# Normalising products of a fused attention and dense kernel placed on GpSimd or VectorE by the planner, with nine thresholds and a reserve table set anew

## Chip, cores and metric

The kernel runs on one core of one Trainium2 chip. The metric is device time in microseconds (us) of one execution. The engines go by the names of the profile: PE (TensorE, matrix products), PEld (its weight loads), ACT (ScalarE), DVE (VectorE), POOL (GpSimd) and SP (SyncE, which issues most DMAs).

## What is computed

The output mixes an attention and a dense block by a gate that is worked out for each token:

```python
g = sigmoid((x * gate_w).sum(-1, keepdims=True))
a = attention(x, wqkv, wo)         # S=2048, D=640, 32 heads of 20, softmax over all keys
b = (h * tanh(softplus(h))) @ w2   # h = x2 @ w1 + b1, F=1536
out = g * a + (1 - g) * b
```

All inputs and the output are bf16.

## The kernel before

The heads go in eight groups of four (g = 0 to 7), the queries in four chunks of 512 (c = 0 to 3). For each pair of chunk and group there are 16 tiles of 128 keys and four heads, and each of these units is one 128 x 512 block of scores in a bank of PSUM. Three units make a slot; there are 683 slots, and all engines work to the beat of the slots.

In a slot PE makes the three blocks of scores (line 1204), into banks 0 to 2 and 3 to 5 by turns, so that the scores of slot s+2 need the banks of slot s. ACT takes their exponentials in one instruction (line 1226), and writes them into ETS as bf16. In most slots only two of the three blocks go to ACT: the third is taken by DVE, which evicts it from PSUM as a 16-bit integer (line 1271, called an eviction here). Up to four such blocks of one group make a batch, and DVE turns a batch into exponentials with three more steps from SBUF to SBUF (line 1335 fraction, line 1339 product, line 1343 power). PE then multiplies the exponentials with the values (line 1463, PV) and gathers the result of the group in one bank, ACC. When a group is done, DVE copies ACC into OUNG (line 1545), the four rows of sums go out and come back through DMAs and a reciprocal (lines 1548 to 1559), spread over the partitions as BCT, and the normalising product OUNG times BCT is written to OTN or QT (line 1513). There are 32 groups, and one of them, the last, goes in two halves by its own code (lines 1532 to 1538); 31 products are made by line 1513.

Beside this, PE has tasks that share one bank, FB: projections of queries, keys and values (lines 598, 667, 795, 822), the hidden layer (950), its second product (1024), the output projection (1048). The bank is evicted by DVE after each task. ACT also makes 24 tanh (line 983) for the hidden layer, and DVE eight steps of the activation for each (lines 1005 and 1008).

The order of all of this on every engine is fixed before the kernel runs. A planner (class `Plan`, function `attention`) keeps a planned clock for each engine, adds each instruction with a planned cost, and decides from its clocks and from thresholds what comes next: `choose` decides for each slot whether its third block goes to DVE, `work` puts pieces of batches, activations and normalising steps into gaps of DVE, `pick` and the loop over `step` choose PE's tasks by due times, `emit_pv` decides when PV is issued, `fill_up` adds PE work that nobody needs (lines 1204 and 1743 again) where PE would idle. So a threshold changes no instruction's work, but which instruction stands where. At run time every engine works through its own list in order, and waits on semaphores for what its next instruction needs.

The functions that the change touches:

Of the kernel before, what the change touches and what calls it, by code (L numbers as in the profile page):

```python
# [14 lines left out]
ALU = mybir.AluOpType  # L15
# [22 lines left out]
OLD = 3  # L38
# [11 lines left out]
HOP = 0.1  # L50
# [5 lines left out]
STREAM = 0.5  # L56
SPUN = 0.65
EXP_PAIR = 0.908
WIDE = 0.60
QUICK = 0.335  # L60
FAST = 0.335
# [9 lines left out]
CHAIN = 2.6  # L71
# [8 lines left out]
AHEAD = 14  # L80
SPREAD = 3
# [7 lines left out]
CROWD = 1.4  # L89
MARGIN = 2.5  # L90
EAGER = 20
# [6 lines left out]
LAG = 5  # L98
SPARE = 7
WINDOW = 3.41  # L100
CALM = 3
PACKED = 10
PACKED_Q = 15
Q_AT = 100
# [26 lines left out]
WARM = 7  # L131
MORE = 8
# [11 lines left out]
class Plan:  # L144
# [3 lines left out]
    def __init__(self, prefix):  # L148
        self.prefix = prefix
        self.ops = []  # L150
        self.now = {e: 0.0 for e in ENGINES}
        self.kind = None
        self.passes = deque()
        self.queue = 0.0

    def add(self, eng, fn, deps=(), slot=None, cost=0.1, kind="F", tail=None, bulk=0.0):
# [86 lines left out]
def bass_gated_mix__softmax_full_mha__dense_activation_mish__prompt_kernel(  # L243
# [142 lines left out]
    def attention(pl, fast):  # L386
# [56 lines left out]
        def dve(fn, deps=(), cost=0.1, kind="F"):  # L443

            ready = max([pl.now["dve"], *(d.t1 + HOP for d in deps if d is not None)])
            work(ready + (LATER if fast and now["rate"] < BUSY and now["bank"] else SLACK))
            return pl.add("dve", fn, deps, cost=cost, kind=kind)
# [72 lines left out]
        if fast:  # L520
# [457 lines left out]
            def mish(ev, hb, hc, k):  # L978
# [9 lines left out]
                def piece(cost, fn, after=None):  # L988
                    def run():
                        last[0] = pl.add("dve", fn, [last[0]], cost=cost)  # L990
# [289 lines left out]
        def dve_by(fn, deps, cost, slack):  # L1280
# [3 lines left out]
            return pl.add("dve", fn, deps, cost=cost)  # L1284

        def close(batch):
# [15 lines left out]
            def piece(cost, fns, deps, after=None, split=False):  # L1302

                def run(some, each, mark):
                    def go():
                        for sp in some:
                            op = pl.add("dve", fns(sp), deps(), cost=each)
# [57 lines left out]
        def choose(s):  # L1365

            late = max(0.0, pl.now["dve"] - pl.now["act"])
# [132 lines left out]
        def group_done(c, g, step, last):  # L1500
# [11 lines left out]
            def times(src, deps):  # L1512
                oung_free[0] = bc_read[0] = otn_done[(c, g)] = pl.add("dve", lambda e: e.tensor_tensor(
                    otn(c, g, fast), src, BC, ALU.mult), [*deps, *reads()], cost=WIDE)
# [42 lines left out]
            def spread():  # L1557
# [5 lines left out]
                norm.append((WIDE, lambda: times(src, wide), lambda: wide[-1]))  # L1563
# [3 lines left out]
        if fast:  # L1567
# [9 lines left out]
            for g in range(NG):  # L1577
                for c in range(NC):
                    due = slot_of(0, g, 4 * c)
                    if c or g:  # L1580
# [4 lines left out]
                        if g == 0:  # L1585
                            tasks.append(kq_task(0, g, c, slot_of(1, 0, 0) - 5 if c < 2 else Q_AT + Q_STEP * (c - 2)))
# [418 lines left out]
```

## Time and profile before

| What | Value |
|---|---|
| median of 3 runs | 793.59 us (791.81 to 795.25) |
| the profiled execution | 791.41 us, span 789.5 us |
| busy: ACT, DVE, PE, POOL | 773.3, 748.3, 716.4, 8.0 us |
| exponentials of three blocks, of two blocks | 281, 402 |
| mean granted clock of TensorE | 0.999 |

The span runs from the first to the last instruction; 1.9 us of the execution lie around it. "Busy" merges instructions that overlap: an instruction starts before the one ahead of it has drained, so a group's mean duration is longer than the time from one start to the next, and a short wait hides under the drain. A row of the timeline gives start, length, engine, line, operation, tiles and count, and in brackets the idle time before it and what ended that. A row of groups ends with busy time, mean ns of one, and the idle time of the engine before the group.

### The profile page before, as it was taken

The page shows a single profiled execution, that of the slowest core. Times are in us where ns is not written, and L with a number is a line of the kernel's source. Part 1 is how long each engine was busy: PE and PEld are TensorE (multiplying, and loading weights), DVE is VectorE, ACT ScalarE, POOL GpSimd, SP SyncE. Part 2 cuts the span into 40 slices and gives each one's busy share as a digit, 9 for nine tenths or more (in the row PEclk, how much of TensorE's full clock was granted, in tenths as well). Part 3 has the DMA queues.
Part 4 walks back from the last instruction along what each step waited for, and adds up shares of the span by engine and source line. Part 5 has one row for each costly group of instructions (what it writes and reads, how often), then busy time and mean ns, then how long its engine had stood idle before and what let it go on. Part 6 is the DMA issues. An engine that isn't in the chain of part 4 may idle for free.

```text
span 789.5 us, 16459 instructions
## 1 busy us (share of the span) xinstructions
PE 716.4 (91%) x6690; PEld 262.7 (33%) x6690; DVE 748.3 (95%) x1313; ACT 773.3 (98%) x715; POOL 8.0 (1%) x14
## 2 busy tenths in 40 slices
PE   8999999889989888999999889999889899999995
PEld 4333333233323332233323233333333333333332
DVE  4889999999999999999999999999999999999995
ACT  6999999999999999999999999999999999999995
POOL 3000000000000000000000000000000000000000
PEclk9999999999999999999999999999999999999999
DMA  8731310211223221402111131202121213010001
GB/s 194 122 74 56 103 51 15 83 54 59 74 89 111 84 64 45 133 17 64 33 29 52 52 90 36 64 19 61 31 85 49 82 48 85 15 28 24 29 15 39
DMA packets 78184, 48.50 MB, mean 61 GB/s; under 512 B 23965, under 2 KB 73749, under 8 KB 78053
## 3 DMA queue, kind: packets, MB, share of 16 engines
q1 hardware_dynamic: 77700, 47.18, 22.2%
q8 instruction: 56, 0.92, 0.5%
q0 software_dynamic: 112, 0.01, 0.1%
q14 instruction: 28, 0.22, 0.1%
q10 hardware_dynamic: 288, 0.16, 0.1%
HBM read 37.64 MB, written 7.52 MB: 57 GB/s over the span
## 4 chain that ended last, share of the span: by engine, by line
ACT 91%; PE 5%; DVE 2%; DMA 1%; issue 0%; SPq 0%; POOL 0%; POOLq 0%
ACT ETS L1226 89%; ACT REG L983 2%; PE PS L1204 2%; PE PS L1463 1%; ACT W2R L983 1%; DMA WOQ<-in_A_wqkv_dram 1%; PE PS L822 0%; PE PS L598 0%; PE PS L667 0%; PE PS L1048 0%; DVE HB L1054 0%; PE PS L758 0%; PE PS L865 0%; PE PS L950 0%; DVE U L1005 0%
## 5 line engine op out<-in xcount | busy, mean ns | idle before, releaser
L1226 ACT ACTIVATE ETS<-PS 128x1024 bf16<-128x1024 f32 (+1 forms) x683 | 753.9, 1370 | 2.7 <-PE PS L1204 2.7
L1204 PE MATMUL PS<-QT,KT 32*128 32x512 bf16 (+1 forms) x2116 | 268.1, 378 | 55.7 <-ACT ETS L1226 46.3
L1463 PE MATMUL PS<-ETS,V_all 128*21 128x512 bf16 (+1 forms) x1699 | 161.8, 375 | 0.0
L1204 PEld LDWEIGHTS PS<-QT,KT 32*128 32x128 bf16 x2116 | 67.2, 91 | 281.4 <-ACT ETS L1226 254.5
L1271 DVE TENSOR_SCALAR PADS<-PS 128x512 int16<-128x512 f32 x97 | 66.3, 685 | 8.5 <-PE PS L1204 8.2
L1271 DVE TENSOR_SCALAR QT<-PS 128x512 int16<-128x512 f32 x102 | 69.7, 685 | 3.9 <-PE PS L1204 3.3
L1024 PE MATMUL PS<-W2R,HB 128*128 128x320 bf16 x384 | 68.5, 302 | 0.7 <-DVE HB L960 0.5
L1271 DVE TENSOR_SCALAR OTN<-PS 128x512 int16<-128x512 f32 x84 | 57.5, 686 | 0.6 <-PE PS L1204 0.5
L950 PE MATMUL PS<-XB,REG 128*128 128x256 bf16 x360 | 53.6, 275 | 2.3 <-DVE OUTT L1054 1.4
L1463 PEld LDWEIGHTS PS<-ETS,V_all 128*21 128x21 bf16 x1699 | 41.9, 91 | 41.2 <-issue 27.1
L1008 DVE TENSOR_TENSOR U<-U 128x1024 f16<-128x1024 f16 x72 | 49.4, 685 | 0.3
L1024 PEld LDWEIGHTS PS<-W2R,HB 128*128 128x128 bf16 x384 | 30.8, 98 | 32.4 <-issue 19.7
L950 PEld LDWEIGHTS PS<-XB,REG 128*128 128x128 bf16 x360 | 29.2, 97 | 25.8 <-issue 23.4
L960 DVE TENSOR_TENSOR HB<-PS,B1T 128x512 bf16<-128x512 f32 x48 | 32.9, 686 | 0.5 <-PE PS L950 0.3
L1005 DVE TENSOR_SCALAR U<-U 128x1024 f16<-128x1024 f16 x72 | 30.2, 420 | 0.4
L1743 PE MATMUL PS<-KT 128*128 128x512 bf16 x92 | 27.3, 384 | 0.0
L1048 PE MATMUL PS<-WOQ,QT 128*128 128x320 bf16 x128 | 24.5, 303 | 2.3 <-DVE HB L1054 0.6
L1271 DVE TENSOR_SCALAR REG<-PS 128x512 int16<-128x512 f32 x38 | 25.8, 685 | 0.2
L1048 PE MATMUL PS<-WOQ,OTN 128*128 128x320 bf16 x128 | 23.8, 302 | 0.1
L667 PE MATMUL PS<-XB,REG 128*128 128x512 bf16 x80 | 23.0, 383 | 0.2 <-DVE WOQ L676 0.2
L822 PE MATMUL PS<-REG,XB 128*128 128x160 bf16 (+1 forms) x240 | 23.1, 234 | 0.0
L667 PE MATMUL PS<-XB,WOQ 128*128 128x512 bf16 x80 | 22.8, 384 | 0.0
(187 smaller groups left out, 809.0 us busy)
## 6 DMA issues: line engine op xcount, KB each, us to landing
REG<-in_B_w_dram SPq DMA_DIRECT2D x36, 320.0 KB, 3.2
BCT<-SUMS SPq DMA_DIRECT2D x124, 64.0 KB, 2.1
W2R<-in_B_w_dram SPq DMA_DIRECT2D x12, 320.0 KB, 3.5
KT<-KS SPq DMA_DIRECT2D x28, 128.0 KB
QT<-QS SPq DMA_DIRECT2D x112, 20.0 KB
QS<-WOQ SPq DMA_DIRECT2D x16, 128.0 KB, 1.7
KS<-OTN SPq DMA_DIRECT2D x16, 128.0 KB, 1.7
W2R<-in_B_w_dram SPq DMA_DIRECT2D x1, 1920.0 KB, 9.8
```

What stands on the lines that cost most here:

```text
L667: return lambda e, bank: e.matmul(PS[:, bank, :], W[:, f, base:base + P], xt(c)[:, f, :], start=(f == 0), stop=(f == NFT - 1))
L950: return lambda e, bank: e.matmul(PS[:, bank, i * HW:(i + 1) * HW], w1b(n1)[:, f, i * P:(i + 1) * P], xt(c)[:, f, cols], start=(f == 0), s ...
L960: ev = dve(lambda e: e.tensor_tensor(hb, PS[:, bank, :].rearrange("p (i t) -> p i t", i=2), bias, ALU.add), [last, b_load, *guarded, *b_re ...
L1005: return lambda e: e.tensor_scalar(dst, src, *ops)
L1008: return lambda e: e.tensor_tensor(dst, one, two, ALU.mult)
L1024: return lambda e, bank: e.matmul(PS[:, bank, 0:HALF], HB[:, hc % 2, f, t * P:(t + 1) * P], W2[:, f, half * HALF:(half + 1) * HALF], start ...
L1048: return lambda e, bank: e.matmul(PS[:, bank, 0:HALF], otn(c, g, fast)[:, t * P:(t + 1) * P], WOG[:, g, half * HALF:(half + 1) * HALF], st ...
L1204: op = pl.add("pe", lambda e, i=i, g=real(g), tile=tile, j=j, cols=cols, c=c, of_q=of_q: e.matmul(scores(s)[:, i, cols], KT[32 * j:32 * j ...
L1226: e_op[s] = pl.add("act", lambda e: e.activation(ETS[:, s % NETS, 0:n, :], scores(s)[:, 0:n, :], AF.Exp, scale=SCALE, bias=LIFT if fast el ...
L1271: ev = dve_by(lambda e: e.tensor_scalar(block(batch["y"], n, I16), scores(s)[:, 2, :], SCALE * ULPS, BIAS, ALU.mult, ALU.add), [s_op[s], * ...
L1463: lasts[n] = pl.add("pe", lambda e, v=v, j=j, src=src[:, cols], of_q=of_q, count=count: e.matmul(PS[32 * j:32 * j + EW, ACC, of_q], v, src ...
L1743: pl.add("pe", lambda e: e.matmul(PS[:, bank, :], k[:, 0:P], k, start=True, stop=True), [free], cost=PASS, kind="S")
```

## The change

It has three parts.

First, the normalising product of a group (line 1513) can be made by POOL. The planner notes every planned DVE instruction with its end and a mark "L" on those that work from SBUF to SBUF in batches, activations and products (`kind="L"`). After each instruction planned through `dve` or `dve_by`, the new function `settle` looks whether the product that waits next could begin on POOL behind the last marked instruction, when its DMA has landed, and end while DVE's planned list still holds unmarked ones. If so the product goes to POOL, and waits for the DVE instruction just ahead of that point. If not, and 4 us (`AWAIT`) of planned time have gone by since its DMA landed, DVE makes it as before.

Second, nine thresholds get new values: how old an exponential may get before its PV is issued regardless of the scores (`OLD` 3 to 2), how dense PE's stream must be (`STREAM`), the planned cost of closing a batch (`CHAIN`), how early forced tasks of PE are begun (`AHEAD`, `SPREAD`) and other tasks may be brought forward (`EAGER`), how much of DVE's other work counts when a batch is judged tight (`CROWD`), how late tasks may be (`LAG`), and the first slot in which DVE may take a block (`CALM`). The first two tasks of queries for group 0 are due 10 slots (`LEAD`) instead of 5 ahead of their need.

Third, a table with one entry for 8 slots (`NUDGE`) is taken off the planned lateness of DVE in `choose`, which makes it more or less willing to give DVE a block there.

```diff
-OLD = 3
+OLD = 2
-STREAM = 0.5
+STREAM = 0.48
+ASIDE = 1.35
+APART = 0.1
+AWAIT = 4
-CHAIN = 2.6
+CHAIN = 3.0
-AHEAD = 14
-SPREAD = 3
+AHEAD = 20
+SPREAD = 4
-CROWD = 1.4
+CROWD = 1.1
-EAGER = 20
+EAGER = 45
-LAG = 5
+LAG = 14
-CALM = 3
+CALM = 2
+LEAD = 10
+NUDGE = [0, 0, 0, 0, 0, 0, 0, 0, 0, 0, -0.5, 0, 0, 0, 0, 0, 0, 1, 0, 0, 0, 0, 0, 2, 1, 0, 0, 0, 0, 0, 0, 0, 2, 0, 0, 0, 0, -1, 0.5, 3, 0, 1, 0, 0, 0, 0, 0, 0, 1, 0, 0, 0, 0, 0, 0, -1, 0, 0, 0, 0, 2, 2, 0, 0.5, 0, 0, 0, 0, 0, 3, -0.5, -0.5, 2, 0, 1, 0, 0, 0, 0, 0, 0, -0.5, 0.5, 0.5, 1, 3]
...
+        if eng == "dve":
+            self.line.append((at + cost, op, kind == "L"))
...
+        def settle():
+
+            if norm and len(norm[0]) > 3:
+                ready, put = norm[0][3]
+                line = pl.line
+                i = len(line)
+                while i and not line[i - 1][2]:
+                    i -= 1
+                begin = max(ready.t1 + HOP, pl.now["pool"], line[i - 1][0] if i else 0.0)
+                while i < len(line) and line[i][0] <= begin:
+                    i += 1
+                if begin + ASIDE + APART <= pl.now["dve"]:
+                    norm.popleft()
+                    put(line[i - 1][1])
...
-            late = max(0.0, pl.now["dve"] - pl.now["act"])
+            late = max(0.0, pl.now["dve"] - pl.now["act"]) - NUDGE[s // 8]
...
-            def times(src, deps):
-                oung_free[0] = bc_read[0] = otn_done[(c, g)] = pl.add("dve", lambda e: e.tensor_tensor(
-                    otn(c, g, fast), src, BC, ALU.mult), [*deps, *reads()], cost=WIDE)
+            def times(src, deps, eng="dve"):
+                oung_free[0] = bc_read[0] = otn_done[(c, g)] = pl.add(eng, lambda e: e.tensor_tensor(
+                    otn(c, g, fast), src, BC, ALU.mult), [*deps, *reads()], cost=WIDE if eng == "dve" else ASIDE, kind="L")
...
-                norm.append((WIDE, lambda: times(src, wide), lambda: wide[-1]))
+                if fast:
+                    norm.append((WIDE, lambda: times(src, wide), lambda: pl.now["dve"] > wide[-1].t1 + AWAIT and wide[-1],
+                                 (wide[-1], lambda dep: times(src, [*wide, dep], "pool"))))
+                else:
+                    norm.append((WIDE, lambda: times(src, wide), lambda: wide[-1]))
...
-                            tasks.append(kq_task(0, g, c, slot_of(1, 0, 0) - 5 if c < 2 else Q_AT + Q_STEP * (c - 2)))
+                            tasks.append(kq_task(0, g, c, slot_of(1, 0, 0) - LEAD if c < 2 else Q_AT + Q_STEP * (c - 2)))
```

What the planner makes of it is seen in the lists of the engines. Lines of the changed kernel are higher by 25 to 31, so line 1513 of before is 1540, 1204 is 1229, 1271 is 1296, 1335, 1339 and 1343 are 1362, 1366 and 1370, 1463 is 1490, and 1054 is 1079. In both kernels ACT's list has 281 exponentials of three blocks, 402 of two blocks and 24 tanh, in another sequence; DVE's has 401 evictions in both. DVE's list has 31 normalising products before and 18 now; the batches are 113 before and 119 now (line 1335, or 1362). Counted by width, a fraction or a power is 2048 wide in 91 batches before and 89 now, 1024 in 15 and 15, 512 in 7 and 15; the products of line 1339 are 38 of 2048, 121 of 1024 and 7 of 512 before, and 40, 113 and 15 now.

On POOL, from the copy of the gate's weights (line 615) to the end of the kernel, the list of the changed kernel now reads:

```order
L615 COPY REG<-OUTT 128x5
L1540 TENSOR_TENSOR OTN<-OUNG,BCT 128x512 x2
L1701 TENSOR_LOAD FLAG
L1701 ISA x2
L1540 TENSOR_TENSOR OTN<-OUNG,BCT 128x512 x5
L1540 TENSOR_TENSOR QT<-OUNG,BCT 128x512 x6
L1903 TENSOR_TENSOR HB<-PADS,W2R 128x320
```

The 13 rows of line 1540 are new; before, POOL had nothing there but the load of a flag and the last row.

On PE, near slot 17, the list of before had a task of values (line 795), one slot's scores, and at once a task of queries (line 598, XB with WOQ), which uses the same bank:

```order
L1463 MATMUL PS<-ETS,V_all 21x512 x7
L795 MATMUL PS<-REG,XB 128x80 x20
L1204 MATMUL PS<-QT,KT 128x512 x3
L598 MATMUL PS<-XB,WOQ 128x512 x5
L1204 MATMUL PS<-QT,KT 128x512 x6
L1463 MATMUL PS<-KT,V_all 21x512 x3
```

In the changed kernel the same task of queries (now line 623) stands a few slots earlier, and its neighbours are others:

```order
L1229 MATMUL PS<-QT,KT 128x512 x3
L820 MATMUL PS<-REG,XB 128x80 x20
L1229 MATMUL PS<-QT,KT 128x512 x6
L1490 MATMUL PS<-ETS,V_all 21x512 x6
L623 MATMUL PS<-XB,WOQ 128x512 x5
L1229 MATMUL PS<-QT,KT 128x512 x6
L623 MATMUL PS<-XB,REG 128x512 x5
```

Two slots' scores and six matmuls of PV now stand between the task of values and that of queries, where one slot's scores stood.

On DVE, near the end, before the last half group is normalised, the list of before had ended its last batch (line 1343) ahead of the half group's copy (line 1530):

```order
L1339 TENSOR_TENSOR OTN<-OTN 128x2048
L1054 SCALAR_TENSOR_TENSOR W2R<-PS,GATE,XB 128x320
L1343 TENSOR_SCALAR OTN<-OTN 128x2048
L1054 SCALAR_TENSOR_TENSOR W2R<-PS,GATE,XB 128x320
L1513 TENSOR_TENSOR QT<-OUNG,BCT 128x512
L1530 COPY OUNG<-PS 128x256
L1532 STREAM_TRANSPOSE BCT<-OUNG 128x256
```

In the changed kernel a whole batch (three rows of lines 1362, 1366 and 1370) stands behind the half group's product (line 1565):

```order
L1540 TENSOR_TENSOR QT<-OUNG,BCT 128x512
L1557 COPY OUNG<-PS 128x256
L1559 STREAM_TRANSPOSE BCT<-OUNG 128x256
L1560 RECIPROCAL RR<-BCT 128x8
L1561 STREAM_TRANSPOSE BCT<-RR 128x256
L1565 TENSOR_TENSOR QT<-OUNG,BCT 128x256
L1362 TENSOR_SCALAR OTN<-REG 128x2048
L1079 SCALAR_TENSOR_TENSOR W2R<-PS,GATE,XB 128x320
L1366 TENSOR_TENSOR OTN<-OTN,REG 128x2048
L1079 SCALAR_TENSOR_TENSOR HB<-PS,GATE,W2R 128x320
L1370 TENSOR_SCALAR REG<-REG 128x2048
```

So one more batch is worked off in the last ten slots, and the block it needs is evicted later than the last one was before.

More of the change, by code (lines that the diff above doesn't have):

```diff
@@ L153, in __init__ @@
         self.passes = deque()
+        self.line = []
         self.queue = 0.0
@@ L989, in run @@
                     def run():
-                        last[0] = pl.add("dve", fn, [last[0]], cost=cost)
+                        last[0] = pl.add("dve", fn, [last[0]], cost=cost, kind="L")
                         if after:
@@ L1306, in go @@
                         for sp in some:
-                            op = pl.add("dve", fns(sp), deps(), cost=each)
+                            op = pl.add("dve", fns(sp), deps(), cost=each, kind="L")
                         if mark:
```

8 lines of the change are left out of this document (6 added, 2 removed).

## The prediction

> **What bounds the kernel now.** First the busy time of each engine, from the page, and the chain of work that ended last:
>
> ```profile
> PE 716.4 (91%) x6690; PEld 262.7 (33%) x6690; DVE 748.3 (95%) x1313; ACT 773.3 (98%) x715; POOL 8.0 (1%) x14
> ACT 91%; PE 5%; DVE 2%; DMA 1%; issue 0%; SPq 0%; POOL 0%; POOLq 0%
> ```
>
> ACT is busy for 773.3 of 789.5 us, and 91% of the last chain is ACT: from its first exponential on the kernel is as long as ACT's list. DVE, with 748.3 us, is the next. So the first question is whether the change shortens ACT's list. These are its groups by form, from the view of groups:
>
> ```profile
> L1226 ACT ACTIVATE ETS<-PS 128x1536 bf16<-128x1536 f32 x281 | 446.9, 1621 | 2.2 <-PE PS L1204 2.2
> L1226 ACT ACTIVATE ETS<-PS 128x1024 bf16<-128x1024 f32 x402 | 441.5, 1194 | 0.5 <-PE PS L1204 0.5
> L983 ACT ACTIVATE REG<-HB 128x1024 f32<-128x1024 bf16 x18 | 22.3, 1239 | 0.0
> L983 ACT ACTIVATE W2R<-HB 128x1024 f32<-128x1024 bf16 x6 | 7.3, 1220 | 0.0
> ```
>
> The durations there overlap (1.621 and 1.194 us hold the drain), so I take the time from start to start. The timeline of ACT has two stretches between tanh, and the groups of these stretches tell what is in them:
>
> ```profile
> 458.18 1.07 ACT L983 ACTIVATE REG<-HB 128x1024 f32<-128x1024 bf16 x1
> 459.13 9.16 ACT L1226 ACTIVATE ETS<-PS 128x1536 bf16<-128x1536 f32 x8
> 468.06 1.17 ACT L983 ACTIVATE REG<-HB 128x1024 f32<-128x1024 bf16 x1
> 469.01 7.43 ACT L1226 ACTIVATE ETS<-PS 128x1536 bf16<-128x1536 f32 x6
> 476.14 1.24 ACT L983 ACTIVATE REG<-HB 128x1024 f32<-128x1024 bf16 x1
> ...
> L1226 ACT ACTIVATE ETS<-PS 128x1536 bf16<-128x1536 f32 x4 | 6.0, 1508 | 0.0
> L1226 ACT ACTIVATE ETS<-PS 128x1024 bf16<-128x1024 f32 x4 | 4.4, 1095 | 0.0
> ...
> L1226 ACT ACTIVATE ETS<-PS 128x1536 bf16<-128x1536 f32 x4 | 6.1, 1595 | 0.0
> L1226 ACT ACTIVATE ETS<-PS 128x1024 bf16<-128x1024 f32 x2 | 2.4, 1178 | 0.0
> ```
>
> From 459.13 to 468.06 four of each kind take 8.93 us, and from 469.01 to 476.14 four long and two short ones take 7.13 us. The difference gives 0.90 us for a short one, and (7.13 - 1.80) / 4 = 1.33 us for a long one; a tanh takes 459.13 - 458.18 = 0.95 us. The whole list is then 281 x 1.3325 + 402 x 0.90 + 24 x 0.95 = 374.4 + 361.8 + 22.8 = 759.0 us without a wait. What does it take? The first exponential and the starts of two later runs:
>
> ```profile
> 9.49 19.26 ACT L1226 ACTIVATE ETS<-PS 128x1536 bf16<-128x1536 f32 x17 [1.05 <-PE PS L1204]
> 29.00 1.45 ACT L1226 ACTIVATE ETS<-PS 128x1536 bf16<-128x1536 f32 x1 [0.25 <-PE PS L1204]
> 31.20 22.28 ACT L1226 ACTIVATE ETS<-PS 128x1536 bf16<-128x1536 f32 x20 [0.75 <-PE PS L1204]
> ...
> 155.08 1.20 ACT L983 ACTIVATE W2R<-HB 128x1024 f32<-128x1024 bf16 x1
> ...
> 690.23 90.37 ACT L1226 ACTIVATE ETS<-PS 128x1024 bf16<-128x1024 f32 x83
> ...
> L1226 ACT ACTIVATE ETS<-PS 128x1024 bf16<-128x1024 f32 x82 | 83.7, 1131 | 0.5 <-PE PS L1204 0.5
> L1226 ACT ACTIVATE ETS<-PS 128x1536 bf16<-128x1536 f32 x51 | 77.0, 1541 | 2.0 <-PE PS L1204 2.0
> ```
>
> The last run ends at 780.60; less the drain of its last instruction (1.19 - 0.90 = 0.29) that is 770.8 us after 9.49. **So ACT loses 770.8 - 759.0 = 11.8 us by waits**, of which 1.7 show as idle (2.2 + 0.5 in the groups, less the 1.05 ahead of the first) and the rest hides under drains. This is all that a new order can win while the list stays. The last two rows are the groups of the first stretch, to 155.08: 51 x 1.3325 + 82 x 0.90 = 141.8 us of work in 145.6 us, a loss of 3.8 us in 133 slots, 0.029 each. The other 550 slots lose 8.0 us, 0.0145 each. Head (9.49 us) and end (8.9 us behind the last exponential) are the rest of the span.
>
> **The change, part by part.** ACT's list holds 281, 402 and 24 instructions in the changed kernel too, so its 759.0 us stay, and the term is 0. Everything else acts by the 11.8 us.
>
> The first stretch. The rows around ACT's waits at 29.00 and 31.20, from the timeline:
>
> ```profile
> 27.73 0.90 PE L795 MATMUL PS<-REG,XB 128*128 128x80 bf16 x20
> 28.56 0.39 PE L1204 MATMUL PS<-QT,KT 32*128 32x512 bf16 x3
> 29.03 0.49 DVE L803 CAST V_all<-PS 128x320 bf16<-128x320 f32 x1
> 29.58 1.25 PE L598 MATMUL PS<-XB,WOQ 128*128 128x512 bf16 x5 [0.62 <-DVE V_all L803]
> 30.76 0.60 PE L1204 MATMUL PS<-QT,KT 32*128 32x512 bf16 x6
> ```
>
> PE stands before the task of queries for 0.62 us, until DVE has emptied the bank, then spends 1.25 us on it, and the scores behind it come at 30.76, for which ACT waits 0.75. In the new list two slots' scores and PV stand between the tasks, so that the bank is empty by then: this wait goes. What is late next is the next task with five matmuls (1.25 us, under a long exponential's 1.33), so not all comes back. Bounds for this stage, with its new AHEAD, SPREAD, LEAD and CALM: nothing gained, or the stretch falls to the rate of the others, 133 x 0.0145 = 1.9 us, a gain of 1.9. From 29.00 to 31.20 ACT made one long exponential, so that wait cost 2.20 - 1.33 = 0.87 us with its hidden part; I take it whole and a third of the other 1.0, -1.2.
>
> DVE's list loses 13 products and gains small pieces. The rows for that:
>
> ```profile
> L1513 DVE TENSOR_TENSOR OTN<-OUNG,BCT 128x512 bf16<-128x512 f32 x16 | 10.9, 684 | 0.0
> L1335 DVE TENSOR_SCALAR OTN<-OTN 128x512 int16<-128x512 int16 x2 | 0.6, 287 | 0.0
> L1343 DVE TENSOR_SCALAR PADS<-PADS 128x2048 int16<-128x2048 int16 x23 | 15.8, 688 | 0.1
> L1339 DVE TENSOR_TENSOR OTN<-OTN 128x1024 f16<-128x1024 f16 x20 | 13.7, 687 | 0.0
> L1339 DVE TENSOR_TENSOR QT<-QT,PADS 128x2048 f16<-128x2048 f16 x4 | 4.9, 1223 | 0.1
> L1339 DVE TENSOR_TENSOR OTN<-OTN 128x512 f16<-128x512 f16 x2 | 0.8, 420 | 0.0
> ```
>
> 13 x 0.684 = 8.9 us go. Fractions and powers: 2 x (8 x 0.287 - 2 x 0.688) = 1.8 us come; products of batches: 2 x 1.223 + 8 x 0.420 - 8 x 0.687 = 0.3 us come. Net 6.8 us less, of 748.3. What is that worth on ACT? One stage by engine (columns PE, PEld, DVE, ACT, POOL):
>
> ```profile
> 600.00:700.00 100.00, 90.94 (x814) 35.94 (x812) 99.30 (x181) 100.00 (x90) 0.00 (x0) 1.00 0.20 55
> ```
>
> DVE is as full as ACT there; an eviction that is late there holds the scores of the slot after next, and so ACT. But ACT's loss is small all the same (8.0 us over all later slots), as each wait covers only what the drains don't. Bounds: 0, where the load of DVE is not what makes the scores late, and -6.8, where each microsecond that DVE saves comes back on ACT. The nearest row is the later stretch's own loss of 0.0145 us a slot, which is near 0; I take -1.2, 15% of the 8.0.
>
> POOL gets the 13 products. The trace has one product of two f32 inputs on POOL, and DVE's mixes beside it:
>
> ```profile
> 782.63 2.09 DVE L1054 SCALAR_TENSOR_TENSOR HB<-PS,GATE,W2R 128x320 bf16<-128x320 f32 x4
> 783.74 0.86 POOL L1872 TENSOR_TENSOR HB<-PADS,W2R 128x320 bf16<-128x320 f32 x1 [759.48 <-ACT PADS L1870]
> ```
>
> 0.86 us for 320 columns is 1.38 for 512, beside DVE instructions that read PSUM and that keep their pace (four in 2.09 us). A result on POOL comes 0.7 us later than on DVE, for a group whose output is needed many slots on: nobody waits. What can cost is a run of evictions that ends before the product. Evictions follow each other at 0.60 us, as these two starts show:
>
> ```profile
> 25.43 0.68 DVE L1271 TENSOR_SCALAR KT<-PS 128x512 int16<-128x512 f32 x1
> 26.03 0.68 DVE L607 CAST KT<-PS 128x512 bf16<-128x512 f32 x1
> ```
>
> Two of them cover 1.2 to 1.3 us of 1.38, so that a product may run on by 0.1 to 0.3 us beside a step from SBUF to SBUF. Bounds: 0, and 13 x 0.3 = 3.9 us of DVE time. I take +0.3 on ACT, near 0, as a shift of DVE of this size is hidden like the rest.
>
> The end. One more batch stands on DVE behind the last half group but one. These rows are DVE's idle time there:
>
> ```profile
> 776.52 0.55 DVE L1054 SCALAR_TENSOR_TENSOR HB<-PS,GATE,W2R 128x320 bf16<-128x320 f32 x1 [0.98 <-PE PS L1048]
> 779.21 0.55 DVE L1054 SCALAR_TENSOR_TENSOR HB<-PS,GATE,W2R 128x320 bf16<-128x320 f32 x1 [2.13 <-PE PS L1048]
> ```
>
> The batch needs 0.69 + 1.22 + 0.69 = 2.6 us, and 0.98 + 2.13 = 3.1 us are free. It is hidden if nothing else is late, and costs up to its last step and a PV (0.69 + 0.39) if it is. I take 0. The other thresholds (OLD, STREAM, CROWD, EAGER, LAG, the table) have no row of their own. They set which slots lose; their bounds are those of the 11.8 us, and I take 0 for them together.
>
> **Sum:** 0 - 1.2 - 1.2 + 0.3 + 0 = -2.1 us. The profiled execution took 791.41 (span 789.5 and 1.9 around it), so its like would take 789.3. The median of before is 793.59, 2.2 above that execution; on the median's footing I forecast **791.5 us**.
>
> **The rivals.**
>
> *DVE was what held the scores.* For it: 99.3 of 100 us busy. Against it: before most exponentials ACT's wait is too short to show. If all 6.8 us come back, and the 1.2 of the first stretch, the time is 793.59 - 8.0 = 785.6; with half of them it is 789. It decides from the point where DVE falls behind by more than the drain of an exponential (0.29 us).
>
> *The products on POOL stop DVE.* If a product starts late or takes longer than 1.38 us, it stands beside a step from SBUF to SBUF; if one of them waits for the other, DVE's list, evictions in it, moves back, PE's scores wait, and ACT. The point is an overrun larger than the drain of 0.29 us. With a whole instruction of 0.69 us for each of the 13, DVE loses 9.0 us. If the half of that shows on ACT and the first stretch gains nothing, the time is 793.59 + 4.5 = 798.1, slower. Against it: the planner places the product beside evictions from PSUM, and the row at 782.63 shows such instructions undisturbed. The Trainium skill ("SBUF — State Buffer", "Who interferes with whom") states that VectorE and GpSimd share a pair of SBUF ports, which one instruction holds whole while the other is fully blocked, where VectorE reads two inputs from SBUF or works in a two-port mode; it would make each overrun a stop until the product's end. No row of this trace shows such a pair. By that rule an overrun of 0.3 us costs 0.3 us, not an instruction.
>
> *The change does nothing that can be seen.* The waits move from slot to slot and their sum stays: 793.6, from the counts of ACT alone. For it: the changed list has as many exponentials of each kind.
>
> **How the numbers follow.** The forecast, from -4 to 0, has a chance of 0.5; the first rival 0.25; nothing to see, or a little slower, 0.12; the second rival 0.13. The range runs from half of DVE's gain with all of the early one and some of the hidden waits (793.59 - 7.1 = 786.5) to the second rival's 798.1, rounded to 798. A measurement of this kernel tells about 0.5% from no change, 4.0 us. Faster by more, below 789.6, is the first rival and the edge of the forecast, 0.28; slower by more, above 797.6, is the second rival with a little, 0.15; the rest is 0.57.
>
> **What would show it.** In the profile of the changed kernel the counts 281, 402 and 24 stay, and ACT's stretch from the first exponential to the last is 768 to 770 us. The wait of 0.75 before line 1226's successor near 31 us is gone. DVE's busy time is near 741.5. Thirteen products on POOL take 1.4 us each, with an L1362, L1366 or L1370 beside them no longer than elsewhere. If the products are longer than 1.7 us, or those rows' maxima above 1.3 us, the second rival is at work. If DVE's busy time falls as told and ACT's stretch stays at 771, DVE was not what held the scores. What would make the prediction wrong is a new wait that the old list did not have, above all at the end, where the last batch comes late.

## The result and the profile after

The changed kernel takes **797.53 us** (median of 14 runs, 795.48 to 798.86) against 793.62 for the kernel before beside it (14 runs, 791.49 to 796.44): ratio 1.0043, 95% interval 1.0030 to 1.0055, so it is slower, by 3.9 us between the medians and by 2.4 to 4.4 us by the interval. The profiled execution took 797.69 us, with a span of 795.9.

The page of the changed kernel, the busy times and the chain of work that ended last:

```profile
PE 716.0 (90%) x6676; PEld 265.3 (33%) x6717; DVE 742.0 (93%) x1314; ACT 774.2 (97%) x715; POOL 24.2 (3%) x27
ACT 88%; DVE 4%; PE 4%; DMA 2%; issue 0%; SPq 0%; POOL 0%; ACTq 0%; POOLq 0%
```

DVE's busy time fell by 6.3 us and ACT's grew by only 0.9, yet the span grew by 6.4. The groups of ACT by form, and POOL's products:

```profile
L1251 ACT ACTIVATE ETS<-PS 128x1536 bf16<-128x1536 f32 x281 | 440.7, 1592 | 3.8 <-PE PS L1229 3.5
L1251 ACT ACTIVATE ETS<-PS 128x1024 bf16<-128x1024 f32 x402 | 435.6, 1169 | 4.2 <-PE PS L1229 4.1
...
L1540 POOL TENSOR_TENSOR OTN<-OUNG,BCT 128x512 bf16<-128x512 f32 x7 | 8.9, 1268 | 333.2 <-DVE QT L1370 79.5 <-DVE KT L1370 72.0 <-DVE HB L1033 69.7
L1540 POOL TENSOR_TENSOR QT<-OUNG,BCT 128x512 bf16<-128x512 f32 x6 | 7.6, 1269 | 383.5 <-DVE REG L1370 339.1 <-DVE QT L1362 22.5 <-DVE PADS L1296 22.0
```

The counts 281 and 402 stand, and ACT's idle time ahead of its exponentials is 8.0 us where it was 2.7. The timeline of ACT tells where; these are its first exponential, the rows that begin with an idle time (in brackets) up to 60 us, and its last run:

```profile
9.40 14.82 ACT L1251 ACTIVATE ETS<-PS 128x1536 bf16<-128x1536 f32 x13 [1.05 <-PE PS L1229]
24.54 3.71 ACT L1251 ACTIVATE ETS<-PS 128x1536 bf16<-128x1536 f32 x3 [0.33 <-PE PS L1229]
28.42 21.00 ACT L1251 ACTIVATE ETS<-PS 128x1024 bf16<-128x1024 f32 x20 [0.17 <-PE PS L1229]
51.60 1.45 ACT L1251 ACTIVATE ETS<-PS 128x1536 bf16<-128x1536 f32 x1 [2.18 <-PE PS L1229]
56.04 1.02 ACT L1251 ACTIVATE ETS<-PS 128x1024 bf16<-128x1024 f32 x1 [3.00 <-PE PS L1229]
57.84 72.71 ACT L1251 ACTIVATE ETS<-PS 128x1024 bf16<-128x1024 f32 x66 [0.77 <-PE PS L1229]
...
690.84 96.03 ACT L1251 ACTIVATE ETS<-PS 128x1024 bf16<-128x1024 f32 x89
```

The wait of 0.75 us at 31.20 is gone, and there are three new ones, 2.18 + 3.00 + 0.77 = 5.95 us between 48 and 58 us. From 9.40 to 690.84 + 96.03 = 786.87 ACT takes 777.5 us; before it was 780.60 - 9.49 = 771.1. The 6.4 us between them are these waits and half a microsecond more.

**What ACT waited for.** The rows of DVE, PE and SP around the waits, each from the engine's timeline, and the longest wait of SP's queue between 30 and 60 us:

```profile
48.42 0.25 DVE L1579 RECIPROCAL RR<-RR 128x16 f32<-128x16 f32 x1 [2.82 <-DMA RR<-OUNG]
50.33 1.28 DVE L1296 TENSOR_SCALAR PADS<-PS 128x512 int16<-128x512 f32 x2
...
51.16 0.39 PE L1229 MATMUL PS<-QT,KT 32*128 32x512 bf16 x3 [2.47 <-DVE PADS L1296]
55.39 0.61 PE L1229 MATMUL PS<-QT,KT 32*128 32x512 bf16 x3 [3.08 <-DMA KT<-KS]
...
29.36 1.78 SPq L651 DMA_DIRECT2D QT<-ZEROS  x4
36.93 0.35 SPq L659 DMA_DIRECT2D QS<-WOQ  x1
38.72 0.62 SPq L1575 DMA_DIRECT2D RR<-OUNG  x1
48.24 1.41 SPq L683 DMA_DIRECT2D QT<-QS  x4
49.69 0.83 SPq L659 DMA_DIRECT2D KS<-OTN  x2
51.44 1.14 SPq L683 DMA_DIRECT2D KT<-KS  x2
...
SPq L227 <- DMA QT<-ZEROS: 8.5, 1, 8.5
```

Read them from the DMA. At 29.36 SP issues the zero store QT<-ZEROS (line 651): four transfers of 336 KB each that clear the unused rows of QT for groups 1 to 7. RR<-OUNG, 8 KB with the sums of the first group, is issued at 38.72 and lands only when DVE's reciprocal starts, at 48.42. DVE, which works in order, stands for 2.82 us in front of it, with two evictions behind; PE's scores wait for those banks, and ACT for the scores. The second wait has the same root. The fetch QT<-QS of group 1 has the zero store among its dependencies (in `fetch`, line 683), so SP stands until the zeros have landed at 48.24; the keys' stores KS<-OTN and their fetch KT<-KS stand behind it in SP's list, KT lands at 55.4, and group 1's first scores need it. The third is PE after both: its matmuls take 0.61 us instead of 0.39. The windows of 5 us (last three columns: granted clock of TensorE, DMA share, GB/s) show clock and transfer:

```profile
30.00:35.00 5.00, 4.77 (x68) 2.27 (x61) 4.77 (x11) 5.00 (x6) 0.00 (x0) 1.00 0.75 101
35.00:40.00 5.00, 4.55 (x35) 1.26 (x39) 4.95 (x10) 5.00 (x6) 0.00 (x0) 1.00 0.81 95
40.00:45.00 5.00, 4.27 (x38) 1.21 (x35) 4.99 (x9) 5.00 (x5) 0.00 (x0) 1.00 0.80 83
...
55.00:60.00 5.00, 4.61 (x46) 2.13 (x46) 2.91 (x6) 3.19 (x3) 0.00 (x0) 0.58 0.20 63
```

The zero store is no part of the change, and its place in SP's list is the same. **Theory:** the new list needs the sums and group 1's keys earlier than the old one, and earlier than the zero store lets them land. **Rival:** the new list is worse in many places, or its products on POOL are, and these waits only happen to be the visible part.

### The profile page after: what moved, and what is told of

Its sections match the earlier page's. It is cut to its first block, busy times and chain, and to the rows that moved or that the text cites. A ratio compares the mean times of both kernels' runs of the same rounds, so it can differ in the third digit from the quotient of the medians.

```text
span 795.9 us, 16515 instructions
## 1 busy us (share of the span) xinstructions
PE 716.0 (90%) x6676; PEld 265.3 (33%) x6717; DVE 742.0 (93%) x1314; ACT 774.2 (97%) x715; POOL 24.2 (3%) x27
## 4 chain that ended last, share of the span: by engine, by line
ACT 88%; DVE 4%; PE 4%; DMA 2%; issue 0%; SPq 0%; POOL 0%; ACTq 0%; POOLq 0%
ACT ETS L1251 86%; ACT REG L1008 2%; DMA RR<-OUNG 1%; PE PS L1229 1%; PE PS L1490 1%; ACT W2R L1008 1%; DMA WOQ<-in_A_wqkv_dram 1%; DMA KT<-KS 0%; PE PS L1073 0%; DVE W2R L1296 0%; PE PS L623 0%; DVE HB L1079 0%; DVE QT L1296 0%; PE PS L820 0%; PE PS L1049 0%
## 5 line engine op out<-in xcount | busy, mean ns | idle before, releaser
L1251 ACT ACTIVATE ETS<-PS 128x1024 bf16<-128x1024 f32 (+1 forms) x683 | 754.2, 1343 | 8.0 <-PE PS L1229 7.7
L1490 PE MATMUL PS<-ETS,V_all 128*21 128x512 bf16 (+1 forms) x1695 | 164.7, 375 | 0.0
L1296 DVE TENSOR_SCALAR QT<-PS 128x512 int16<-128x512 f32 x97 | 65.9, 681 | 4.7 <-PE PS L1229 4.2
L1296 DVE TENSOR_SCALAR OTN<-PS 128x512 int16<-128x512 f32 x89 | 60.6, 683 | 2.9 <-PE PS L1229 2.5
L1296 DVE TENSOR_SCALAR PADS<-PS 128x512 int16<-128x512 f32 x71 | 48.5, 684 | 7.4 <-PE PS L1229 7.1
L1296 DVE TENSOR_SCALAR REG<-PS 128x512 int16<-128x512 f32 x60 | 40.6, 680 | 2.7 <-PE PS L1229 2.5
L1296 DVE TENSOR_SCALAR KT<-PS 128x512 int16<-128x512 f32 x34 | 23.2, 682 | 7.4 <-PE PS L1229 7.3
L1296 DVE TENSOR_SCALAR W2R<-PS 128x512 int16<-128x512 f32 x32 | 21.7, 681 | 1.1 <-PE PS L1229 1.1
```

The source lines that it names most:

```text
L1251: e_op[s] = pl.add("act", lambda e: e.activation(ETS[:, s % NETS, 0:n, :], scores(s)[:, 0:n, :], AF.Exp, scale=SCALE, bias=LIFT if fast el ...
L1296: ev = dve_by(lambda e: e.tensor_scalar(block(batch["y"], n, I16), scores(s)[:, 2, :], SCALE * ULPS, BIAS, ALU.mult, ALU.add), [s_op[s], * ...
L1490: lasts[n] = pl.add("pe", lambda e, v=v, j=j, src=src[:, cols], of_q=of_q, count=count: e.matmul(PS[32 * j:32 * j + EW, ACC, of_q], v, src ...
```

## The experiments

Unless said otherwise a ratio is to the kernel before, run on the same chip in the same set (medians 795.38, 795.2, 795.0 and 794.6 us in the four sets).

**The changed kernel again, with the products put back, and with the zero store cut.** Three kernels and one of before:

```diff
 # a_dve: behind the planning, the 13 products go back to DVE, at their places in the list
+    for op in fast.ops:
+        if op.eng == "pool" and op.fn.__code__.co_freevars and "BC" in op.fn.__code__.co_freevars and "src" in op.fn.__code__.co_freevars:
+            op.eng = op.key = "dve"
 # a_split, b_split: QT<-ZEROS clears group 1 alone (4 x 48 KB); three later lots, each behind
 # a set of BCT spreads, clear groups 2, 3 to 4, and 5 to 7; the fetches of a group wait for its lot
-                        QT[32 * j + DH:32 * j + 32, 1:NG, :],
...
+                        QT[32 * j + DH:32 * j + 32, 1:2, :],
...
+    for n, (a, b) in enumerate(((2, 3), (3, 5), (5, 8))):
...
```

> The changed kernel as it is, profiled a second time. Theory Z (the zeros for the query rows, 4 x 336 KB on SP's queue, land late, and hold the first reciprocal on DVE and the first fetch of keys): two waits of ACT between 48 and 58 us come again, together 4 to 7 us, and the time is 3 to 5 us above before. Rival C (chance in the arrival of the first DMAs, this profile alone): the waits are gone or under 2 us in this profile.

Measured: 798.83 us, 1.0042 (1.0025 to 1.0059). The waits came again, 2.44 and 3.10 us in its profile.

> The changed kernel with the 13 products of GpSimd made by VectorE, each at the place in its list where the planner would have begun it on GpSimd; all else as planned. DVE gets 8.9 us of work back. Theory D (DVE's load holds the scores): 3 to 9 us slower than the changed kernel. Theory N (DVE's load is not what holds ACT): within 1 us of the changed kernel.

Measured: 800.39 us, 1.0056 (1.0034 to 1.0078), 1.6 us above the repeat by the medians, between the two theories; the two sets of runs overlap (797.54 to 800.32 and 798.71 to 801.01). The products on POOL are not the loss: without them the kernel is no faster.

> The changed kernel with the same list on every engine but SP: the zeros of group 1 alone are written first (4 x 48 KB), those of groups 2 to 7 in three lots behind the first three spreads of BCT. Theory Z: the waits of ACT between 48 and 58 us fall from 6.5 us to under 1.5, and the kernel is 5 to 6.5 us faster than the changed one, about 791 to 792, 2 us faster than before. Rival O (the new order asks for the keys and the reciprocal too early whatever the DMAs do): the waits stay above 4 us, the time stays near 797.

Measured: 797.84 us, 1.0028 (1.0014 to 1.0041): 1.0 us less than the repeat, not the gain that the theory asked for. But the profile shows why. ACT's timeline up to 120 us, and the rows of SP and DVE at its new wait:

```profile
28.72 84.95 ACT L1256 ACTIVATE ETS<-PS 128x1024 bf16<-128x1024 f32 x78 [0.17 <-PE PS L1234]
117.25 1.02 ACT L1256 ACTIVATE ETS<-PS 128x1024 bf16<-128x1024 f32 x1 [3.58 <-PE PS L1234]
119.52 11.51 ACT L1256 ACTIVATE ETS<-PS 128x1024 bf16<-128x1024 f32 x10 [1.25 <-PE PS L1234]
...
96.27 1.62 SPq L1989 DMA_DIRECT2D QT<-ZEROS  x4
97.93 0.35 SPq L662 DMA_DIRECT2D KS<-OTN  x1
109.66 1.11 SPq L686 DMA_DIRECT2D KT<-KS  x2
...
115.87 0.25 DVE L1584 RECIPROCAL RR<-RR 128x16 f32<-128x16 f32 x1 [4.93 <-DMA RR<-OUNG]
```

All three waits at the head are gone: from 28.72 to 113.67 ACT runs without a gap. The third lot of zeros (4 x 144 KB, issued at 96.27) makes the same trouble again: the store KS<-OTN behind it lands only at 109.66, SP stands, RR<-OUNG is issued late, and DVE waits 4.93 us. So the theory's mechanism held twice, and the sum hid it.

> The kernel before with the zeros written in the same four lots. Theory Z: before has the same bottleneck in small (PE idle 1.1 us, ACT waits 0.3 to 0.6 us near 53 us in the profile seen, more in slower runs), so 0.5 to 2.5 us faster than before. Rival O: no difference, within 0.5 us.

Measured: 796.83 us, 1.0012 (0.9998 to 1.0026), so the gain that was expected did not come; its lots cost 1.80 and 0.92 us of ACT's idle time at 105 and 121 us.

**The kernel before once more, and the zero store earlier in both.** The second edit moves instructions that exist:

```diff
 # a_early, b_early: on POOL the store of the zero row ahead of two loads, on SP QT<-ZEROS ahead of KS<-ZEROS
+    for mover, goal in (("zero", "b1"), ("qz", "kz")):
+        moved = [op for op in fast.ops if op.slot == mover]
...
+        fast.ops[:] = [op for op in fast.ops if op.slot != mover]
+        at = min(i for i, op in enumerate(fast.ops) if op.slot == goal)
+        fast.ops[at:at] = moved
```

> The kernel before, unchanged, with a profile of another execution. In its first profile the zero store was issued at 27.1 us, in the profiles of the changed kernel at 28.0 to 29.7. If that start is only the luck of an execution (the three transposes of x end 2 us earlier or later) and the first reciprocal is close to its data in this list too, then a start near 29.3 us makes VectorE wait some 2 us for RR<-OUNG near 46 to 48 us, ScalarE waits 1.5 to 2 us behind it, and the span is 791 to 793 us. If the old list has room there, ScalarE waits less than 0.6 us between 45 and 60 us however late the zero store is, and the span stays within 789 to 790 us.

Measured: 794.84 us, span 793.0, against 789.5 in the profile that the prediction used. Rows of SP, DVE and ACT:

```profile
29.26 1.78 SPq L626 DMA_DIRECT2D QT<-ZEROS  x4
48.64 1.42 SPq L658 DMA_DIRECT2D QT<-QS  x4
...
48.82 0.25 DVE L1552 RECIPROCAL RR<-RR 128x16 f32<-128x16 f32 x1 [2.54 <-DMA RR<-OUNG]
...
50.20 1.45 ACT L1226 ACTIVATE ETS<-PS 128x1536 bf16<-128x1536 f32 x1 [1.70 <-PE PS L1204]
52.12 1.02 ACT L1226 ACTIVATE ETS<-PS 128x1024 bf16<-128x1024 f32 x1 [0.47 <-PE PS L1204]
53.55 13.51 ACT L1226 ACTIVATE ETS<-PS 128x1536 bf16<-128x1536 f32 x12 [0.40 <-PE PS L1204]
```

The old list pays too, 1.70 + 0.47 + 0.40 = 2.57 us, when the zero store starts 2.1 us later. That start is not in the list: it follows the three transposes of x, for which POOL, ahead of its store of the zero row, waited 8.7 us in the first profile, 10.6 in this one and 10.7 in that of the changed kernel.

> The changed kernel with the zero store earlier: POOL issues the store of the zero row ahead of the loads of B1T and of the gate, and SyncE issues QT<-ZEROS ahead of KS<-ZEROS; no other instruction moves. Theory of the zero store (the loads that the first reciprocal and the first fetches need stand behind its 1.3 MB): QT<-ZEROS starts some 5 us earlier, RR<-OUNG lands ahead of its reciprocal at 45 us, ScalarE's three waits of 2.4, 3.1 and 0.8 to 0.9 us between 48 and 60 us go, and the kernel gains 5 to 7 us on a repeat of itself (798.8): 792 to 794 us, 0.5% faster than it and 0.1 to 0.4% faster than before. Rival, that the new list is slower in many small places: the three waits may go, but the gain is under 2 us, because what is late next takes it.

Measured: 794.35 us, 0.9987 (0.9970 to 1.0004), 4.5 us less than the repeat; a difference to the kernel before is not shown. The runs spread: five lie from 791.3 to 792.8, seven from 793.9 to 796.6.

> The changed kernel with the early zero store once more, for the profile of a second execution: the first was at 790.1 us with a zero store that began at 20.9 us, under the median of its runs. If the start of the zero store still decides, a later start (23 to 24 us) shows a wait for KT<-KS of 2 to 4 us near 51 us, and a span of 792 to 794 us.

Measured: 791.95 us, span 790.1, with a start at 21.23 us: another execution like the first, so what holds the slower seven up is not shown.

> The kernel before with the same two moves. If the zero store costs the old list something in most executions, it gains 1 to 2.5 us; if the old list has room there, it is within 0.5 us of the kernel before (0.1%).

Measured: **792.96 us, 0.9962 (0.9949 to 0.9975)**, 2.2 us less than the kernel before beside it. So the late zeros cost the old list something in most executions, too.

**Which of the two things at the head, and which part of the change.** In a_swap the four fetches QT<-QS go behind the keys' stores and fetches in SP's list. The other three are the changed kernel's code with other numbers: in a_calm `CALM = 3`; in a_nonudge a table of zeros; in a_pool all nine thresholds and `LEAD` as before and a table of zeros, so that the products on POOL (10 in this plan) are the only part left.

> The changed kernel with one move in SyncE's list: the four fetches QT<-QS of group 1, which wait for the zero store to land, stand behind the two KS<-OTN stores and the two KT<-KS fetches instead of ahead of them. If the wait of 3.0 us for KT<-KS near 55 us is the queue (the K path stood issued behind an instruction that waits for the zeros), KT<-KS is issued some 3 to 5 us earlier, that wait shrinks to under 1 us and the drop of the clock behind it goes: 3 to 4 us less than the changed kernel, the reciprocal's wait of 2.2 to 2.4 us stays. If it is the transfers themselves (the zeros hold the DMA rings, whoever is issued first), KT<-KS still lands at 54 us or later and the gain is under 1 us.

Measured: 797.47 us, 1.0030 (1.0017 to 1.0042), by the ratios 1.0 us less than the changed kernel: neither of the two cases as told. The fetch of the keys is issued at 47.08 us instead of 51.44 and no longer waited for; its place is taken by the fetch that it changed places with, in this row of PE:

```profile
53.12 0.61 PE L1229 MATMUL PS<-QT,KT 32*128 32x512 bf16 x3 [2.38 <-DMA QT<-QS]
```

So the order of the two fetches in SP's list is not the cause: both must have landed, and one of them can't be issued before the zeros have landed.

> The changed kernel with one of the nine thresholds put back (CALM 3 instead of 2). In the list that comes out, group 1's first score tile stands in slot 41 instead of 38, 9 tiles or 4 us of exponentials later; the first reciprocal keeps its place in VectorE's list. If the head of the list is the loss, the wait for KT<-KS goes and the one for the reciprocal stays: 3 to 4 us less than the changed kernel. The rest of the list moves too, and the reserve table was fitted to the other one: if the end goes wrong as in the run with old thresholds and products on GpSimd (ScalarE idle for 11.5 us ahead of the last additions), it is slower by up to 10 us instead, while the head's waits are still gone.

Measured: 807.58 us, 1.0152 (1.0126 to 1.0177). With the old `CALM` ACT has no idle time between 31 and 120 us of its profile, so the wait for the keys hangs on this threshold. The wait for the reciprocal was expected to stay and is gone as well; but QT<-QS was issued at 46.47 us here and the reciprocal started at 46.65, so whether it comes back with a later landing is not shown. And the end falls apart, as it does in the next two.

> The changed kernel with the reserve table all zero, thresholds and products on GpSimd as they are. The list up to slot 80 is the same, so the three waits between 48 and 60 us stay (6 to 8 us). If the table is what keeps the end in order, ScalarE idles several us at the end (2.6 us with it): 2 to 10 us slower than the changed kernel. If the table does nothing that shows, the same within 1 us.

Measured: 806.84 us, 1.0151 (1.0127 to 1.0174), by the ratios 8.6 us more than the changed kernel; the waits at the head stay, 5.56 us.

> The code of the changed kernel with the old nine thresholds, the old due time of the two projections of Q and an empty reserve table, so that products on GpSimd are the only part that is left. SyncE's list begins as before's does. If the loss is the thresholds' new head of the list, this is 0 to 2 us faster than before (0.9975 to 1.0000): putting the 13 products back on VectorE cost the changed kernel 1.6 us. If products on GpSimd are what costs, it is 2 to 4 us slower than before (1.0025 to 1.005).

Measured: 805.60 us, 1.0131 (1.0114 to 1.0147), which neither case of the expectation has: the waits at the head are down to 1.77 us, and the loss is at the end. ACT's row behind the last exponential in the changed kernel, in a_calm, in a_nonudge and in a_pool:

```profile
789.46 0.53 ACT L1901 ACTIVATE PADS<-PS,GATE 128x320 f32<-128x320 f32 x1 [2.59 <-PE PS L1073]
```
```profile
800.81 0.53 ACT L1901 ACTIVATE PADS<-PS,GATE 128x320 f32<-128x320 f32 x1 [13.69 <-PE PS L1073]
```
```profile
797.44 0.53 ACT L1901 ACTIVATE PADS<-PS,GATE 128x320 f32<-128x320 f32 x1 [9.02 <-PE PS L1073]
```
```profile
795.67 0.53 ACT L1901 ACTIVATE PADS<-PS,GATE 128x320 f32<-128x320 f32 x1 [11.53 <-PE PS L1073]
```

And the mixes of the output (line 1079, on DVE) behind the last exponential, from a_nonudge and from the changed kernel, counted by the windows with that line alone:

```profile
788.40:804.00 15.60, 4.21 (x8) 0.66 0.17 48
```
```profile
786.90:796.00 9.10, 2.56 (x5) 0.84 0.26 73
```

Five are left for the end in the changed kernel (and before), eight without the table, ten in a_pool and in a_calm. With the old numbers, or a part of them, PE's last tasks are undone when the exponentials end; in the changed kernel the thresholds and the table together keep that from happening. That the table was fitted to this one list is a reading of these three runs, not a test.

**The head freed.** Early store as above, for group 1 alone, and the other six groups one by one (192 KB) behind the first six sets of BCT spreads.

```diff
+    for g, n in zip(range(2, NG), [3, 7, 11, 15, 19, 23]):
...
+        at = fast.ops.index(spreads[n]) + 1
+        fast.ops[at:at] = lot
```

> The changed kernel with the early zero store, which now clears group 1 alone (4 x 48 KB); groups 2 to 7 follow one by one (192 KB each), behind the first six sets of BCT spreads. If the head of the list is the whole loss, its waits are gone in every execution (early zeros alone still spread from 791.3 to 796.6 us, in two clusters) and no later lot holds a load for over 1 us: 790 to 792.5 us, 0.3 to 0.6% faster than before. If the list is worse elsewhere too, it stays above 794 us.

Measured: **791.16 us (790.87 to 791.99), 0.9955 (0.9942 to 0.9968)**, the fastest here. ACT's rows from 26 to 130 us:

```profile
25.82 2.36 ACT L1256 ACTIVATE ETS<-PS 128x1536 bf16<-128x1536 f32 x2
28.35 102.27 ACT L1256 ACTIVATE ETS<-PS 128x1024 bf16<-128x1024 f32 x94 [0.17 <-PE PS L1234]
```

Neither the three waits nor the one of a_split that ended at 117.25 us are left in this profile, and the five runs lie within 1.1 us, where the 14 of the changed kernel lay within 3.4.

> The kernel before with the same lots and the early store. It lost 0.4 to 3 us at the head, and 2 to 3 us with the coarser lots at 102 and 120 us: 791.5 to 793.5 us if the finer lots hold no load. With the head freed in both, the new list with products on GpSimd should be 1 to 2.5 us faster than this one, if the rest of the change is worth what the prediction's terms said (2.1 us); if the two are within 0.5 us, the rest is worth nothing.

Measured: 792.35 us (790.96 to 792.92), 0.9963 (0.9949 to 0.9977), 1.2 us above a_fine by the medians; the two sets of runs overlap.

> The changed kernel with the lots and the early store, and its 13 products on VectorE at their places in the list. Against the kernel with the lots and products on GpSimd this prices the move alone without the head's waits in the way: 1 to 2 us slower (it was 1.6 us with them); 0 if VectorE's 13 x 0.52 us of extra work lies in idle time.

Measured: 791.93 us (791.59 to 792.59), 0.9963 (0.9950 to 0.9976), 0.8 us above a_fine, a little less than expected.

These runs price the head in both lists. By the ratios to the kernel before, freeing it brought the changed kernel from 1.0043 to 0.9955, some 7.0 us, and the kernel before from 1 to 0.9963, some 2.9 us. The difference, 4.1 us, is more than the changed kernel's loss by its ratio (0.43%, 3.4 us): with the head freed in both, the changed kernel is no slower. As these edits move only the zero stores and the loads around them, and leave the lists of PE, ACT and DVE alone, this shows the cause; a list that is worse in many places, or the products on POOL, would have kept the loss.

## Why the prediction was wrong

The forecast was 791.5, 6.0 us too low, and on the wrong side of no change. That the measured time lies inside the range at all, half a microsecond below its upper end of 798, is luck: this end was set for the second rival, which did not cause the loss. The earliest QT<-QS waits for the zero store to land, and up to 1.2 us more for the store QS<-WOQ behind it. Set beside the time at which SP issued it, ACT's idle time between 45 and 62 us reads:

| Kernel | list | QT<-QS issued, us | ACT idle, us |
|---|---|---|---|
| b_early | old | 45.6 | 0 |
| before | old | 46.2 | 0.28 |
| a_pool | old | 46.8 | 1.77 |
| b_again | old | 48.6 | 2.57 |
| a_calm | new, `CALM` 3 | 46.5 | 0 |
| a_early | new | 43.4 | 0.40 |
| a_early2 | new | 43.5 | 0.73 |
| a_nonudge | new | 47.2 | 5.56 |
| changed | new | 48.2 | 5.95 |
| a_again | new | 48.4 | 7.16 |
| a_dve | new | 48.4 | 7.09 |

("Old" for a_pool means its thresholds; its products are on POOL.) At the same time of issue the new list pays 3 to 5 us more than the old, and it is nearly free of waits near 43 us where the old one is so near 46. That is the size of the loss.

- *"Bounds for this stage, with its new AHEAD, SPREAD, LEAD and CALM: nothing gained, or the stretch falls to the rate of the others"*, taken as -1.2. **This is the step that failed.** The bounds had no loss in them. The wait at 31 us went, as told (0.33 and 0.17 us came at 24 and 28 us instead), but what was late next was a transfer and not the next task of PE. DVE came to the first reciprocal at 45.60 us (48.42 - 2.82), 0.7 us earlier than the old list in b_again, and PE to group 1's scores at 52.31 us, 3.08 us ahead of their keys. So waits of 5.95 us stand where 1.2 us were to be gained; by the runs with the head freed, the new head costs some 4.1 us more than the old one. Of the thresholds in it, `CALM` alone was put back; the share of the others is open. The row was there, though not under ACT. In the first profile SP stood 5.6 us for QT<-ZEROS, and QT<-QS went out 0.2 us ahead of the reciprocal:

```profile
SPq L219 <- DMA QT<-ZEROS: 5.6, 1, 5.6
46.22 1.41 SPq L658 DMA_DIRECT2D QT<-QS  x4
46.41 0.25 DVE L1552 RECIPROCAL RR<-RR 128x16 f32<-128x16 f32 x1
```

The old list had no room at all there, and a list that asks earlier had to pay. I looked for terms only where ACT waited.
- *"The other thresholds (OLD, STREAM, CROWD, EAGER, LAG, the table) have no row of their own ... and I take 0 for them together."* Of these only the table was taken out by itself, and it is not worth nothing: without it the kernel is 8.6 us slower. What the others do one by one was not tried.
- *"The profiled execution took 791.41 ... on the median's footing".* Right as arithmetic, but the 2.2 us between execution and median were no constant: a good part of them was this same wait. The profiled execution paid 0.28 us of it and b_again 2.57, and moving the zero store (b_early) took 2.2 us off the median.
- *DVE's 6.8 us less work, -1.2, and the products on POOL, +0.3.* DVE's busy time fell by 6.3. Products on POOL took 1.27 us for an estimate of 1.38. Putting them back costs 1.6 us (a_dve against a_again) or 0.8 (a_fine_dve against a_fine), with runs that overlap: of the size told.
- *The end, 0.* Its wait is 2.59 us, before 2.52, so the term held. But the table and the thresholds hold it there; in the three runs without a part of them this wait is 6 to 11 us longer.
- *The sum without the head.* With both heads freed, the new list is at 791.16 and the old at 792.35: 1.2 us, where my terms gave 2.1. The two sets of runs overlap, so a gain is likely and its size open.
- *What would show it.* The counts, the wait at 31 us and DVE's busy time (742.0 for 741.5) came as told; ACT's stretch took 777.5 us instead of 768 to 770. The prediction named a new wait as what would make it wrong, but looked for it at the end, and it came at the head.
- *First rival, DVE held the scores.* It fell: 5.0 us more of DVE's busy time in a_dve and 5.3 in a_fine_dve cost 1.6 and 0.8 us.
- *Second rival, products on POOL stop DVE.* It came true for one product of the 13, and is not the loss. Most products stand like this one, on POOL and on DVE:

```profile
224.80 1.26 POOL L1540 TENSOR_TENSOR OTN<-OUNG,BCT 128x512 bf16<-128x512 f32 x1 [69.67 <-DVE HB L1033]
```
```profile
224.57 0.68 DVE L1296 TENSOR_SCALAR PADS<-PS 128x512 int16<-128x512 f32 x1
225.17 0.68 DVE L701 CAST WOQ<-PS 128x512 bf16<-128x512 f32 x1
```

The evictions from PSUM keep their 0.68 us. Beside eleven others DVE has instructions that read PSUM too, once a reduction of one row besides (0.65 us, before 0.66), or nothing at all. But one product stands beside a step from SBUF to SBUF, the first of the sigmoid (line 872), which the planner doesn't mark "L". These are the product and the step in the changed kernel, and the same step in a_dve, where the product is on DVE:

```profile
297.57 1.27 POOL L1540 TENSOR_TENSOR OTN<-OUNG,BCT 128x512 bf16<-128x512 f32 x1 [19.84 <-DVE QT L1366]
297.95 0.93 DVE L872 TENSOR_SCALAR OMG<-GATE 128x16 f32<-128x16 f32 x1
```
```profile
299.49 0.17 DVE L872 TENSOR_SCALAR OMG<-GATE 128x16 f32<-128x16 f32 x1
```

The step takes 0.93 us instead of 0.17 and ends with the product, at 298.88 and 298.84 us. Soon after it PE waits 0.63 us for a bank (0.23 in a_dve), and ACT 0.18 us at 301.22. It is the same in a_again and a_fine (0.93 and 0.92 us), and 0.16 us in a_fine_dve. The Trainium skill ("SBUF — State Buffer", "Who interferes with whom") states that of two such instructions the one that issues first gets the shared ports for its whole length and the other is fully blocked; the trace agrees. As a_fine has this stop too and is the fastest kernel here, it is no part of the loss to speak of.

Open: what each threshold does by itself; how much of the difference of 3.9 us between the medians is the list and how much the mixture of executions; and why the transposes of x end 2 us apart.

## What to carry over

A wait of zero in one profile can be a margin of 0.2 us. Before a list is made tighter, look for what each early load stands behind in the DMA queue, even where no engine waits yet, and take a second profile. A large transfer that nobody needs at once (here zeros for all later groups, the last of which is fetched at 314 us) is cut to the part that is needed and put where it holds nothing; cut into lots that are still too large it only moves the wait. Thresholds that were set for one list are one part with it: with a part of them undone the kernel took 1.3 to 1.5% more than before. And who places work of POOL beside DVE marks every step of DVE from SBUF to SBUF, the short ones too: the one that was left out took five times as long.

## What the hardware showed besides

- While the zero store ran, the DMA share stood at 0.75 to 0.81 with 83 to 101 GB/s, though the same engines moved 274 GB/s at a share of 0.98 between 20 and 25 us; a 128 KB store (QS<-WOQ) issued behind it took 11.3 us to land, and 1.7 us in a_fine. The transfers have 12 rows each. The Trainium skill ("DMA: Bandwidth & Descriptors", "Why a DMA increments its semaphore by 16 and not by 1") states that a DMA issued by SP runs on the largest number of engines up to 16 that divides the slowest dimension of both sides, 12 here; 12 of 16 is 0.75, and the trace agrees. Its section "Queues, rings and completion order" has each engine take one queue's work in order, which is what the small loads show.
- TensorE's granted clock fell to 0.58 between 55 and 60 us (in windows of 1 us it reads 0.50 from 53 to 59), and its matmuls took 0.61 us for 0.39. It fell near 52.3 us, 1.2 us behind a gap of PE of 2.47 us; in a_again near 51.1 us, within a gap of 2.52; in b_again near 50.2 us, 0.4 us behind a gap of 1.95. The Trainium skill's page "TensorE: Matmul & The Clock Gate" ("Part 1: The HAM clock gate") puts the gate at an idle window of about 3.4 us that runs freely, and half rate. The half rate agrees; gaps of 1.95 to 2.52 us were enough here.
